# Re-ordering the opening of an adaLN, linear-attention and GLU block: two issuing engines, and the modulation sums of two column blocks on TensorE

## The chip, the cores and the metric

The kernel runs on one core of one Trainium2 chip. The metric is the device time of one execution in microseconds (us), as the median of several runs. Engines are called by their names or as the profile writes them: TensorE (PE for matmuls, PEld for weight loads), VectorE (DVE), ScalarE (ACT), GpSimd (POOL) and SyncE (SP).

## The reference

One transformer block over x of 2048 tokens by 512 columns in float32, with a modulation by a conditioning vector c of 512 numbers:

```
mod = silu(c) @ w_mod                       # 6 x 512: sa, ca, ga, sb, cb, gb
h = layernorm(x) * (1 + ca) + sa
q, k, v = split(h @ wqkv)                   # 32 heads of 16
pq, pk = phi(q), phi(k)                     # phi(t) = (t + 1 if t > 0 else exp(t)) + 1e-6
o = pq (pk^T v) / (pq . sum(pk))            # linear attention, per head
x = x + ga * (o @ wo)
h = layernorm(x) * (1 + cb) + sb
x = x + gb * (((h @ w_gate) * (h @ w_up)) @ w_down)   # inner width 1376
```

The opening, which the change re-orders, covers the layer norm of the first 512 tokens, sa and ca (the "shift" and the "scale" of the first norm), the transposes, the modulation, and the key product of the first four token tiles.

## The kernel before

The 2048 tokens are four chunks of four tiles of 128 tokens. The 512 columns are four blocks of 128 (KD = 4, index k or b). All instructions of an engine run in the order in which the program writes them, and each engine runs its own list; semaphores order them where they share data. DMAs are issued in the program's order by the engine that issues them, and eight completion semaphores are used in turn, so that an issue waits for the transfer eight places ahead of it.

Float32 products are made of two reduced parts. A matrix is split into a high part (a cast on ScalarE) and a low part (the difference, on VectorE), and each product is three matmuls: high by high, high by low, low by high.

The opening goes like this:

- SyncE issues, in this order, x tile 0, c (`ct`), x tiles 1 to 3, the first halves (column blocks 0 and 1) of scale and shift of `w_mod`, the first key weight, the second halves (column blocks 2 and 3), the other three key weights, then x of chunk 1 and the weights of q and v. Each of these tiles is 256 KB, and c is 2 KB. In `raw_half[v, half]`, v = 1 is the scale and v = 0 the shift.
- TensorE has nothing to do until the first tokens are normed. `keep_on(n)` gives it n matmuls of 128x512 on zeros into `ps_idle`, which nobody reads.
- `silu` makes `sc` from c. `n0.stats`, `rstd_of`, `nmr_of` and `xhat` norm the four token tiles (VectorE, a power on GpSimd, then ScalarE or VectorE).
- `transpose_token(j)` turns token tile j, one matmul for each column block, into the four banks `n0.ps[k]`.
- The column sums of silu(c) by `w_mod` are made in one of two ways for each column block b. `block_pe(v, b)` is four matmuls with one output column, accumulated over the four rows of c. `half_dve(v, half, ...)` sums the four pieces on VectorE for two blocks at once, and then `block_one(v, b)` sums over the partitions by one matmul against ones. `block_out(b)` adds 1 to the scale's column and brings the two columns of block b to SBUF. A one-column matmul stands as two records in the profile.
- `mod_h(k)` and `mod_f(k)` (ScalarE) make the high part and the float32 form of the modulated block k from `n0.ps[k]`, and `mod_l(k)` (VectorE) the low part. `weight_h(k)` and `weight_l(k)` split the key weight of row block k. `k_split_xh` and `k_split_xl` split the normed tokens, which are wanted later by `t_tile`.
- `cells((t, k), ..., parts=...)` is the key product: token tile t, row block k, and which of the three matmuls (part 0 high by high, 1 the weight's low part, 2 the tokens' low part). There are 48 in all, L444.

Behind `cells` stands `proj(0, wq)` (its first matmul is L211), and from there on the kernel is a long list of products. The lines of the profile that belong to these steps: L154 `keep_on`, L283 `transpose_token`, L393 `block_pe`, L170 and L172 the sums of `half_dve`, L404 `block_one`, L408 `block_out`, L415 `mod_h`, L422 `mod_f`, L427 `mod_l`, L432 `weight_h`, L435 `weight_l`, L242 `stats`, L254 the power of `rstd_of`, L259 `nmr_of`, L269 `xhat`.

Of the kernel before, what the change touches and what calls it, by code (L numbers as in the profile page):

```python
# [9 lines left out]
F32R = mybir.dt.float32r  # L10
AF = mybir.ActivationFunctionType
# [3 lines left out]
P = 128  # L15
# [7 lines left out]
def tile_adaln_block(  # L23
# [12 lines left out]
    nc = tc.nc  # L36
# [3 lines left out]
    KD = D // P  # L40
    NJ = 4
# [8 lines left out]
    xv = x[0].rearrange("(c p j) d -> c j p d", p=P, j=NJ)  # L50
# [14 lines left out]
    def f32(ap):  # L65
        return ap.bitcast(F32)
# [3 lines left out]
    def T(p, tag, shape=(P, D), dt=F32, bufs=None):  # L70
        cnt[0] += 1
        return p.tile(list(shape), dt, tag="t" if p is tiles else tag, name=f"{tag}_{cnt[0]}", bufs=bufs)

    def B(tag, shape=(P, D), dt=F32):

        return T(tiles, tag, shape, dt)

    def acc_bank():
        return T(ps_acc, "acc")

    def bank():
        return T(ps_w, "bank")
# [23 lines left out]
    nc.gpsimd.memset(half, -0.5)  # L106


    def load(src, tag):
        raw = B(tag, (P, *src.shape[1:]))[:src.shape[0]]  # L110
        nc.sync.dma_start(raw, src)
        return raw

    def load_x(ch):
        return [load(xv[ch, j], "x") for j in range(NJ)]

    def load_mod(v):
        return [load(wm_v[:, k, v * D:(v + 1) * D], "raw") for k in range(KD)]

    def load_half(v, half):  # L120
        a = v * D + half * D // 2
        return [load(wm_v[:, k:k + 2, a:a + D // 2], "raw") for k in range(0, KD, 2)]
# [3 lines left out]

    xts = [[load(xv[0, 0], "x")]]
    ct = consts.tile([P, KD], F32, name="ct")
    nc.sync.dma_start(ct, c[0].rearrange("(p k) -> p k", k=KD))
    xts[0] += [load(xv[0, j], "x") for j in range(1, NJ)]  # L130
    raw_half = {}
    raw_half[1, 0] = load_half(1, 0)
    raw_half[0, 0] = load_half(0, 0)
    load_k = lambda k: load(wqkv_v[k, :, D:2 * D], "raw")
    raw_k = [load_k(0)]
    raw_half[1, 1] = load_half(1, 1)
    raw_half[0, 1] = load_half(0, 1)
    raw_k += [load_k(k) for k in range(1, KD)]
    xts.append(load_x(1))
    raw_q = load_qkv(0)  # L140
    raw_v = load_qkv(2)
# [8 lines left out]
    ps_idle = T(ps_acc, "acc")  # L150

    def keep_on(n):
        for _ in range(n):
            nc.tensor.matmul(ps_idle, idle[:, :P], idle, start=True, stop=True)  # L154
# [3 lines left out]
    sc = consts.tile([P, KD], F32, name="sc")  # L158
# [8 lines left out]
    def mod_acc(acc, raws, ks):  # L167
        for k in ks:
            if k == 0:
                nc.vector.tensor_scalar(acc, raws[k], sc[:, 0:1], None, op0=ALU.mult)  # L170
            else:
                nc.vector.scalar_tensor_tensor(acc, raws[k], sc[:, k:k + 1], acc, op0=ALU.mult, op1=ALU.add)  # L172
# [133 lines left out]
    def proj(i, w, of=bank):  # L306

        ch, j = divmod(i, NJ)
        ps = of()
        product(ps, [(cut(norm[ch].t[k], j * P, (j + 1) * P), w[k]) for k in range(KD)])  # L310
        return ps
# [9 lines left out]
    def k_split_xh(i):  # L321
        ch, j = divmod(i, NJ)
        kx[i] = [B("xh", dt=F32R), B("xl", dt=F32R)]
        nc.scalar.activation(kx[i][0], norm[ch].n[j], AF.Copy)

    def k_split_xl(i):
        ch, j = divmod(i, NJ)
        nc.vector.tensor_tensor(kx[i][1], norm[ch].n[j], f32(kx[i][0]), op=ALU.subtract)
# [45 lines left out]
    n0 = norm[0]  # L374
    both = consts.tile([P, KD, 2], F32, name="both")
    ca, sa = both[:, :, 0], both[:, :, 1]
    ps_m = acc_bank()

    def half_of(v, b):

        pair = raw_half[v, b // 2]
        return [pair[k // 2][:, k % 2, b % 2 * P:(b % 2 + 1) * P] for k in range(KD)]

    def at_of(v, b):
        return 2 * b + 1 - v

    def sums_in(b):
        return ps_idle if b == 1 else ps_m

    def block_pe(v, b):  # L390
        at, ps = at_of(v, b), sums_in(b)
        for k, raw in enumerate(half_of(v, b)):
            nc.tensor.matmul(ps[:, at:at + 1], raw, sc[:, k:k + 1], start=k == 0, stop=k == KD - 1)  # L393

    sums = {}

    def half_dve(v, half, *ks):
        if 0 in ks:
            sums[v, half] = B("f")[:, :D // 2]
        mod_acc(sums[v, half], [raw_half[v, half][k // 2][:, k % 2] for k in range(KD)], ks)  # L400

    def block_one(v, b):
        at = at_of(v, b)
        nc.tensor.matmul(sums_in(b)[:, at:at + 1], sums[v, b // 2][:, b % 2 * P:(b % 2 + 1) * P], ones,  # L404
                         start=True, stop=True)

    def block_out(b):
        nc.vector.tensor_tensor(both[:, b], sums_in(b)[:, 2 * b:2 * b + 2], unit, op=ALU.add)  # L408

    halves = {}  # L410

    def mod_h(k):
        halves[k] = (B("h", dt=F32R), B("h", dt=F32R), B("f"))
        h, l, f = halves[k]
        nc.scalar.activation(h, n0.ps[k], AF.Identity, scale=ca[:, k:k + 1], bias=sa[:, k:k + 1])  # L415

    def mod_f(k, on=None):
        h, l, f = halves[k]
        if on:
            on.tensor_scalar(f, n0.ps[k], ca[:, k:k + 1], sa[:, k:k + 1], op0=ALU.mult, op1=ALU.add)  # L420
        else:
            nc.scalar.activation(f, n0.ps[k], AF.Identity, scale=ca[:, k:k + 1], bias=sa[:, k:k + 1])  # L422
        n0.ps[k] = None

    def mod_l(k):
        h, l, f = halves.pop(k)
        nc.vector.tensor_tensor(l, f, f32(h), op=ALU.subtract)  # L427
        n0.t[k] = (h, l)

    def weight_h(k):  # L430
        wk.append((B("w", dt=F32R), B("w", dt=F32R)))
        nc.scalar.activation(wk[k][0], raw_k[k], AF.Copy)  # L432

    def weight_l(k, on=None):
        (on or nc.vector).tensor_tensor(wk[k][1], raw_k[k], f32(wk[k][0]), op=ALU.subtract)  # L435
# [3 lines left out]
    def cells(*tk, parts=(0, 1, 2)):  # L439
        for part in parts:  # L440
            for t, k in tk:
                h, l = halves[k][:2] if k in halves else n0.t[k]
                x, w = ((h, wk[k][0]), (h, wk[k][1]), (l, wk[k][0]))[part]
                nc.tensor.matmul(kps[t], x[:, t * P:(t + 1) * P], w, start=k == 0 and part == 0,  # L444
                                 stop=k == KD - 1 and part == 2)
# [7 lines left out]
    n0.stats(2)  # L453
    n0.nmr_of(0, 2)
    n0.xhat(0, 1)
    k_split_xh(0)
    n0.stats(3)
    n0.rstd_of(2, 4)
    n0.transpose_token(0)
    n0.nmr_of(2, 4)  # L460
    n0.xhat(2)
    n0.xhat(3, on=nc.vector)
    keep_on(2)
    n0.transpose_token(1)
    block_pe(1, 0)
    keep_on(1)
    half_dve(0, 0, 0, 1, 2, 3)
    weight_h(0)
    n0.transpose_token(2)
    n0.transpose_token(3)  # L470
    keep_on(2)
    block_one(0, 0)
    block_out(0)
    weight_l(0)
    mod_h(0)
    mod_f(0)
    block_pe(1, 1)
    block_one(0, 1)
    half_dve(1, 1, 0, 1)
    block_out(1)  # L480
    half_dve(1, 1, 2, 3)
    mod_l(0)
    kps.update({t: acc_bank() for t in range(2)})
    kps[2] = ps_idle
    kps[3] = bank()
    four = lambda k: [(t, k) for t in range(NJ)]
    cells((0, 0), (1, 0), parts=(0, 1))
    cells((2, 0), (3, 0), parts=(0, 1))
    cells(*four(0), parts=(2,))
    mod_h(1)  # L490
    mod_f(1)
    weight_h(1)
    half_dve(0, 1, 0, 1, 2, 3)
    weight_l(1)
    mod_l(1)
    k_split_xh(1)
    cells(*four(1), parts=(0,))
    block_one(1, 2)
    block_one(0, 2)
    block_one(1, 3)  # L500
    block_one(0, 3)
    cells(*four(1), parts=(1, 2))
    weight_h(2)
    block_out(2)
    block_out(3)
    weight_l(2)
    mod_h(2)
    mod_f(2)
    weight_h(3)
    mod_l(2)  # L510
    mod_h(3)
    weight_l(3)
    mod_f(3)
    k_split_xl(0)
    mod_l(3)
    cells((0, 2), (1, 2))
    cells((2, 2))
    cells((0, 3))
    cells((3, 2))
    cells((1, 3))  # L520
    cells((2, 3))
    cells((3, 3))
    k_split_xl(1)
    nx = Norm(xts[1])

# [18 lines left out]
    ps_m = None  # L544
# [75 lines left out]
    for i in range(4, NT):  # L620
        ch, j = divmod(i, NJ)
# [122 lines left out]
    ps = proj(6, wq)  # L744
# [35 lines left out]
    ps = proj(8, wq)  # L780
# [8 lines left out]
    ps = proj(9, wq)  # L789
# [5 lines left out]
    ps = proj(10, wq)  # L795
# [3 lines left out]
    ps = bank()  # L799
# [583 lines left out]
    for n, (s, g, f) in enumerate(order):  # L1383
# [7 lines left out]
        at = {p: list(early.get((n, p), ())) for p in ("a11", "s1", "s2", "s3", "mid", "s4", "pe")}  # L1391
# [140 lines left out]
```

## Time and profile before

| what | value |
|---|---|
| median of 3 runs | 556.27 us (556.25 to 557.45) |
| the profiled execution, its own time | 557.03 us |
| its span, first to last instruction | 555.0 us |
| busy: TensorE, VectorE, ScalarE, GpSimd | 547.7, 420.4, 296.0, 178.3 us |
| mean granted TensorE clock | 0.998 |
| moved by DMA | 83.75 MB |

The span is the stretch between the first and the last instruction of the profiled execution; its own time has about 2 us around that. The busy times are unions over one engine. In a timeline row, the columns are the start and the length in us, the engine, the line of the kernel, the operation, the tiles (output, then inputs), the shapes, how many instructions are merged into the row, and in brackets the idle time ahead of it and what ended it. In a row by stretch, the first number after the stretch is its length, then for each engine (PE, PEld, DVE, ACT, POOL, or TensorE alone) its busy time with the number of instructions, then the granted clock, the share of the DMA engines, and GB/s.

### The profile page before, as it was taken

The numbers are of one execution on the slowest core, as the hardware profiler recorded it, in microseconds if no ns is written. First come the engines' busy times: TensorE is split into PE (matmuls) and PEld (weight loads), VectorE is DVE, ScalarE is ACT, GpSimd is POOL, SyncE is SP. The second block draws the span as 40 slices with busy tenths as digits, with TensorE's granted clock in tenths as the row PEclk, the third lists the DMA queues.
The fourth block names the chain that finished last, engine by engine and source line by source line (L and its number), as shares of the span: only waits on it lengthen the run. The fifth ranks groups of instructions, "written<-read, shape, count | busy, mean of one in ns | idle before, by whom it ended". The sixth has DMA issues, their size and how long they took to land.

```text
span 555.0 us, 8026 instructions
## 1 busy us (share of the span) xinstructions
PE 547.7 (99%) x2739; PEld 459.8 (83%) x2739; DVE 420.4 (76%) x758; ACT 296.0 (53%) x525; POOL 178.3 (32%) x183
## 2 busy tenths in 40 slices
PE   8999999999999999999999999999999999999996
PEld 6788888888888888888888888878888888888886
DVE  5968779978898998865655767854567878778695
ACT  3876858546467876653545355432443535443540
POOL 2000000002627646343556644400512524242400
PEclk9999999999999999999999999999999999999999
DMA  8910224203230045185888635499585534342004
GB/s 261 384 38 1 76 77 151 78 0 77 77 115 2 0 149 192 39 298 196 284 283 268 227 123 199 154 379 327 176 275 178 185 119 146 131 147 72 0 1 152
DMA packets 56888, 83.75 MB, mean 151 GB/s; under 512 B 6736, under 2 KB 21840, under 8 KB 56848
## 3 DMA queue, kind: packets, MB, share of 16 engines
q1 hardware_dynamic: 56848, 83.26, 43.9%
q8 instruction: 21, 0.34, 0.2%
q14 instruction: 19, 0.16, 0.1%
HBM read 53.54 MB, written 29.69 MB: 150 GB/s over the span
## 4 chain that ended last, share of the span: by engine, by line
PE 96%; DMA 1%; DVE 1%; SPq 0%; issue 0%; ACT 0%; POOL 0%; DVEq 0%
PE bank L1023 38%; PE acc L1182 8%; PE acc L837 8%; PE bank L211 5%; PE bank L213 5%; PE bank L212 5%; PE acc L1106 4%; PE acc L1105 4%; PE acc L1107 4%; PE acc L362 3%; PE acc L361 3%; PE acc L360 3%; PE bank L276 2%; PE acc L444 1%; PE bank L812 1%; DMA x<-in_A_x_dram 1%
## 5 line engine op out<-in xcount | busy, mean ns | idle before, releaser
L1023 PE MATMUL bank<-h,w 128*128 128x512 f32 (+1 forms) x924 | 220.5, 392 | 0.0
L1023 PEld LDWEIGHTS bank<-h,w 128*128 128x128 f32 (+1 forms) x924 | 168.8, 186 | 36.5 <-issue 0.4
L1029 ACT ACTIVATE bank<-bank 128x512 f32<-128x512 f32 (+1 forms) x45 | 26.2, 581 | 131.3 <-PE bank L1023 131.0
L986 POOL TENSOR_TENSOR w<-raw,w 128x256 fp32r<-128x256 f32 (+3 forms) x22 | 24.2, 1099 | 79.7 <-ACT w L979 64.9
L1206 DVE TENSOR_TENSOR x<-acc,x 128x256 f32<-128x256 f32 x108 | 39.2, 414 | 10.5 <-PE acc L1182 9.9
L1182 PE MATMUL acc<-w,kh 128*128 128x256 f32 x252 | 46.8, 283 | 0.0
L211 PE MATMUL bank<-w,h 128*128 128x512 f32 x112 | 44.1, 394 | 0.0
L1182 PEld LDWEIGHTS acc<-w,kh 128*128 128x128 f32 x252 | 41.4, 191 | 3.1 <-DVE x L1206 0.2
L213 PE MATMUL bank<-w,h 128*128 128x512 f32 x112 | 43.7, 390 | 0.0
L212 PE MATMUL bank<-w,h 128*128 128x512 f32 x112 | 43.7, 390 | 0.0
L837 PE MATMUL acc<-w,xh 128*128 128x512 f32 x128 | 40.7, 399 | 0.0
L254 POOL TENSOR_TENSOR rstd<-ve,half 128x4 f32<-128x4 f32 (+3 forms) x12 | 11.2, 930 | 82.7 <-DVE ve L251 71.2
L1049 DVE TENSOR_TENSOR phi<-bank,g 128x512 f32<-128x512 f32 (+1 forms) x22 | 15.1, 687 | 29.8 <-PE bank L1023 28.3
L686 POOL TENSOR_TENSOR f<-h,zb 128x512 f32<-128x512 f32 x12 | 17.5, 1475 | 62.2 <-ACT zb L666 48.8
L1079 DVE TENSOR_TENSOR g<-bank,u 128x512 f32<-128x512 f32 (+1 forms) x22 | 15.2, 690 | 28.0 <-ACT u L1029 26.7
L1106 PE MATMUL acc<-w,kh 128*128 128x512 f32 (+1 forms) x92 | 35.9, 391 | 0.0
L1105 PE MATMUL acc<-w,kh 128*128 128x512 f32 (+1 forms) x92 | 35.9, 391 | 0.0
L1107 PE MATMUL acc<-w,kl 128*128 128x512 f32 (+1 forms) x92 | 35.8, 390 | 0.0
L1182 PE MATMUL acc<-w,kl 128*128 128x256 f32 x126 | 35.7, 283 | 0.0
L1029 ACT ACTIVATE u<-bank 128x512 f32<-128x512 f32 (+1 forms) x44 | 26.2, 594 | 12.6 <-PE bank L1023 12.4
L1112 DVE TENSOR_TENSOR x<-acc,x 128x512 f32<-128x512 f32 x44 | 28.0, 680 | 6.2 <-PE acc L1107 6.2
L269 ACT ACTIVATE n<-x,nmr,rstd 128x512 f32<-128x512 f32 x31 | 23.6, 808 | 14.2 <-DVE nmr L259 14.0
(195 smaller groups left out, 1186.8 us busy)
## 6 DMA issues: line engine op xcount, KB each, us to landing
right<-w SPq DMA_DIRECT2D x56, 256.0 KB, 3.8
w<-right SPq DMA_DIRECT2D x56, 256.0 KB, 3.7
x<-in_A_x_dram SPq DMA_DIRECT2D x24, 256.0 KB, 5.3
raw<-in_w_mod_dram SPq DMA_DIRECT2D x24, 256.0 KB, 3.6
raw<-in_B_w_down_dram SPq DMA_DIRECT2D x20, 256.0 KB, 3.1
side_s<-h SPq DMA_DIRECT2D x16, 256.0 KB, 2.8
h<-side_s SPq DMA_DIRECT2D x16, 256.0 KB, 6.0
raw<-in_A_wqkv_dram SPq DMA_DIRECT2D x12, 256.0 KB, 5.4
```

What stands on the lines that cost most here:

```text
L211: nc.tensor.matmul(ps, ah, bh, start=begin and i == 0, stop=False)
L212: nc.tensor.matmul(ps, ah, bl, start=False, stop=False)
L213: nc.tensor.matmul(ps, al, bh, start=False, stop=end and i == n - 1)
L837: nc.tensor.matmul(yps[i], x, y, start=fresh and k + n == 0, stop=k == KD - 1 and n == 2, skip_group_check=True)
L1023: mm = lambda x, y, **kw: nc.tensor.matmul(ps, x[:, k], y, skip_group_check=True, **kw)
L1029: nc.scalar.activation(out, x, AF.Copy)
L1105: nc.tensor.matmul(dn[j], hh[:n, a:b], dh[:n], start=i == 0, stop=False)
L1106: nc.tensor.matmul(dn[j], hh[:n, a:b], dl[:n], start=False, stop=False)
L1107: nc.tensor.matmul(dn[j], hl[:n, a:b], dh[:n], start=False, stop=i == n_of - 1)
L1112: nc.vector.tensor_tensor(xt, dn[j], xt, op=ALU.add)
L1182: mm = lambda x, y, **kw: nc.tensor.matmul(ps, x[:, a:b], y, skip_group_check=True, **kw)
L1206: nc.vector.tensor_tensor(xt[:, halves[at]], banks[b][:, part], xt[:, halves[at]], op=ALU.add)
```

## The change

- c and x tiles 1 and 3 are issued by ScalarE; x tile 2 and everything else by SyncE.
- The second key weight is issued ahead of the second half of the shift.
- For column block 0 the shift is summed by `block_pe` instead of `half_dve` and `block_one`; for block 1 too, and its four matmuls stand behind the first four cells. All sums go to the bank `ps_m`.
- The unread matmuls behind the first eighteen are three instead of five: one between the transposes of tokens 0 and 1, two ahead of `block_pe(1, 1)` and the first product.
- The transposes of tokens 3 and 2 stand behind the sums of block 0.
- The order of the casts, splits and cells behind that is another: `k_split_xh` comes later, `block_one` of blocks 2 and 3 is split around the second part of k = 1, both `mod_h` of blocks 2 and 3 come ahead of both `mod_f`, and the cells of k = 2 and 3 are ordered by part.
- `mod_h` gets a range of columns, of which only the whole is used.

```diff
-    def load(src, tag):
+    def load(src, tag, by=None):
         raw = B(tag, (P, *src.shape[1:]))[:src.shape[0]]
-        nc.sync.dma_start(raw, src)
+        (by or nc.sync).dma_start(raw, src)
         return raw
...
-    nc.sync.dma_start(ct, c[0].rearrange("(p k) -> p k", k=KD))
-    xts[0] += [load(xv[0, j], "x") for j in range(1, NJ)]
+    nc.scalar.dma_start(ct, c[0].rearrange("(p k) -> p k", k=KD))
+    xts[0] += [load(xv[0, j], "x", by=nc.sync if j == 2 else nc.scalar) for j in range(1, NJ)]
...
     raw_half[1, 1] = load_half(1, 1)
+    raw_k += [load_k(1)]
     raw_half[0, 1] = load_half(0, 1)
-    raw_k += [load_k(k) for k in range(1, KD)]
+    raw_k += [load_k(k) for k in range(2, KD)]
...
     def sums_in(b):
-        return ps_idle if b == 1 else ps_m
+        return ps_m
...
-            nc.tensor.matmul(ps[:, at:at + 1], raw, sc[:, k:k + 1], start=k == 0, stop=k == KD - 1)
+            nc.tensor.matmul(ps[:, at:at + 1], raw, sc[:, k:k + 1], start=k == 0, stop=k == KD - 1,
+                             skip_group_check=True)
...
     n0.xhat(0, 1)
-    k_split_xh(0)
     n0.stats(3)
     n0.rstd_of(2, 4)
     n0.transpose_token(0)
+    keep_on(1)
+    n0.transpose_token(1)
+    block_pe(1, 0)
+    block_pe(0, 0)
     n0.nmr_of(2, 4)
     n0.xhat(2)
     n0.xhat(3, on=nc.vector)
+    block_out(0)
+    weight_h(0)
+    n0.transpose_token(3)
+    n0.transpose_token(2)
     keep_on(2)
-    n0.transpose_token(1)
-    block_pe(1, 0)
-    keep_on(1)
-    half_dve(0, 0, 0, 1, 2, 3)
-    weight_h(0)
-    n0.transpose_token(2)
-    n0.transpose_token(3)
-    keep_on(2)
-    block_one(0, 0)
-    block_out(0)
+    block_pe(1, 1)
+    mod_h(0)
+    half_dve(1, 1, 0, 1)
     weight_l(0)
-    mod_h(0)
     mod_f(0)
-    block_pe(1, 1)
-    block_one(0, 1)
-    half_dve(1, 1, 0, 1)
-    block_out(1)
     half_dve(1, 1, 2, 3)
     mod_l(0)
+    weight_h(1)
...
-    cells((0, 0), (1, 0), parts=(0, 1))
-    cells((2, 0), (3, 0), parts=(0, 1))
-    cells(*four(0), parts=(2,))
+    cells(*four(0), parts=(0,))
+    block_pe(0, 1)
+    block_out(1)
+    cells(*four(0), parts=(1, 2))
     mod_h(1)
+    weight_l(1)
     mod_f(1)
-    weight_h(1)
-    half_dve(0, 1, 0, 1, 2, 3)
-    weight_l(1)
+    half_dve(0, 1, 0)
     mod_l(1)
+    half_dve(0, 1, 1, 2, 3)
+    weight_h(2)
+    weight_h(3)
+    k_split_xh(0)
     k_split_xh(1)
     cells(*four(1), parts=(0,))
     block_one(1, 2)
+    block_one(1, 3)
+    cells(*four(1), parts=(1,))
     block_one(0, 2)
-    block_one(1, 3)
     block_one(0, 3)
-    cells(*four(1), parts=(1, 2))
-    weight_h(2)
+    cells(*four(1), parts=(2,))
     block_out(2)
     block_out(3)
     weight_l(2)
     mod_h(2)
+    mod_h(3)
     mod_f(2)
-    weight_h(3)
+    weight_l(3)
+    k_split_xl(0)
     mod_l(2)
-    mod_h(3)
-    weight_l(3)
     mod_f(3)
-    k_split_xl(0)
     mod_l(3)
-    cells((0, 2), (1, 2))
-    cells((2, 2))
-    cells((0, 3))
-    cells((3, 2))
-    cells((1, 3))
-    cells((2, 3))
-    cells((3, 3))
+    cells(*four(2), parts=(0, 1))
+    for t in range(NJ):
+        cells((t, 3), parts=(0, 1))
+        cells((t, 2), (t, 3), parts=(2,))
```

More of the change, by code (lines that the diff above doesn't have):

```diff
@@ L410, in tile_adaln_block, with mod_h @@
     halves = {}
[L412 to L415, printed above, removed]
+    def mod_h(k, a=0, b=NJ):
+        if not a:
+            halves[k] = (B("h", dt=F32R), B("h", dt=F32R), B("f"))
+        h = halves[k][0][:, a * P:b * P]
+        nc.scalar.activation(h, n0.ps[k][:, a * P:b * P], AF.Identity, scale=ca[:, k:k + 1], bias=sa[:, k:k + 1])
     def mod_f(k, on=None):
```

## The prediction

> **What bounds the kernel now.** I read the page's span and busy line first, then the busy time by stretch, then TensorE's timeline of the first 30 us, and the other engines' timelines only where TensorE was late.
>
> ```profile
> span 555.0 us, 8026 instructions
> PE 547.7 (99%) x2739; PEld 459.8 (83%) x2739; DVE 420.4 (76%) x758; ACT 296.0 (53%) x525; POOL 178.3 (32%) x183
> 5.00:6.00 1.00, 1.00 (x4) 0.71 (x4) 0.89 (x4) 0.00 (x0) 0.00 (x0) 1.00 0.71 204
> ...
> 11.00:12.00 1.00, 0.66 (x5) 0.41 (x5) 0.96 (x3) 0.54 (x1) 0.00 (x0) 1.00 1.09 351
> 30.00:35.00 5.00, 5.00 (x24) 4.14 (x23) 3.74 (x11) 1.86 (x4) 1.01 (x1) 1.00 0.00 1
> ```
>
> TensorE is busy for 547.7 of 555.0 us, and from the first full stage on (30 to 35 us: 5.00 of 5.00) it never waits. The change touches nothing behind that, so the question is only when TensorE reaches `proj(0, wq)`, the first L211. Its opening:
>
> ```profile
> 1.98 6.58 PE L154 MATMUL acc<-w 128*128 128x512 f32 x18 [1.98 <-DVE w L149]
> 8.56 0.66 PE L283 MATMUL bank<-ident,n 128*128 128x128 f32 x4
> ...
> 9.53 0.60 PE L283 MATMUL bank<-ident,n 128*128 128x128 f32 x4
> 9.96 0.95 PE L393 MATMUL acc<-sc,raw 128*128 128x1 f32 x8
> 10.78 0.47 PE L154 MATMUL acc<-w 128*128 128x512 f32 x1
> 11.60 1.09 PE L283 MATMUL bank<-ident,n 128*128 128x128 f32 x8 [0.34 <-ACT n L269]
> 12.45 0.71 PE L154 MATMUL acc<-w 128*128 128x512 f32 x2
> 13.24 0.35 PE L404 MATMUL acc<-ones,f 128*128 128x1 f32 x2
> 13.46 1.03 PE L393 MATMUL acc<-sc,raw 128*128 128x1 f32 x8
> 14.35 0.36 PE L404 MATMUL acc<-ones,f 128*128 128x1 f32 x2
> 14.66 1.43 PE L444 MATMUL acc<-w,h 128*128 128x512 f32 x5
> ...
> 16.38 0.39 PE L444 MATMUL bank<-w,h 128*128 128x512 f32 x1
> 16.89 0.97 PE L444 MATMUL acc<-w,h 128*128 128x512 f32 x3
> ...
> 18.84 0.95 PE L404 MATMUL acc<-ones,f 128*128 128x1 f32 x8
> 19.65 0.94 PE L444 MATMUL acc<-w,h 128*128 128x512 f32 x3
> ...
> 27.20 0.39 PE L211 MATMUL bank<-w,h 128*128 128x512 f32 x1
> ...
> 29.92 0.39 PE L360 MATMUL acc<-kh,xh 128*128 128x512 f32 x1
> ```
>
> The first useful matmul (L444, `cells`) starts at 14.66, L211 at 27.20: 12.54 us for the 48 matmuls of `cells`. Spacing: twelve matmuls from 27.20 to 29.92, 0.227 each. One `block_pe` (four matmuls, two records each) takes 0.82 to 0.89 (9.96 to 10.78, 13.46 to 14.35), four `block_one` 0.81 (18.84 to 19.65), four transposes 0.43 (9.53 to 9.96), eight 0.85 (11.60 to 12.45). So 12.54 is 48 x 0.227 = 10.9, plus 0.81, plus 0.8 of lost time; one loss is visible, 16.38 to 16.89, 0.28 beyond the spacing.
>
> What sets 14.66:
>
> ```profile
> 1.24 0.42 SPq L129 DMA_DIRECT2D ct<-in_c_dram  x1
> 1.71 1.37 SPq L111 DMA_DIRECT2D x<-in_A_x_dram  x3
> 5.48 0.69 DVE L242 BATCH_NORM_STATS2 st<-x 128x6 f32<-128x512 f32 x1
> 6.62 0.70 DVE L242 BATCH_NORM_STATS2 st<-x 128x6 f32<-128x512 f32 x1
> 8.60 0.69 DVE L242 BATCH_NORM_STATS2 st<-x 128x6 f32<-128x512 f32 x1 [0.94 <-DMA x<-in_A_x_dram]
> 11.57 1.52 DVE L172 SCALAR_TENSOR_TENSOR f<-raw,sc,f 128x256 f32<-128x256 f32 x3
> 13.63 0.16 DVE L408 TENSOR_TENSOR both<-acc,unit 128x2 f32<-128x2 f32 x1 [0.54 <-PE acc L404]
> 16.15 0.68 DVE L427 TENSOR_TENSOR h<-f,h 128x512 fp32r<-128x512 f32 x1
> 7.69 1.52 ACT L269 ACTIVATE n<-x,nmr,rstd 128x512 f32<-128x512 f32 x2 [3.39 <-DVE nmr L259]
> 12.30 0.63 ACT L432 ACTIVATE w<-raw 128x512 fp32r<-128x512 f32 x1 [0.76 <-DMA raw<-in_A_wqkv_dram]
> 13.83 0.78 ACT L415 ACTIVATE h<-bank,both 128x512 fp32r<-128x512 f32 x1 [0.89 <-DVE both L408]
> 20.03 0.78 ACT L415 ACTIVATE h<-bank,both 128x512 fp32r<-128x512 f32 x1 [1.72 <-DVE both L408]
> 20.70 0.77 ACT L422 ACTIVATE f<-bank,both 128x512 f32<-128x512 f32 x1
> ```
>
> The transposes of block 0 are done at 12.45, but block 0's shift is summed on VectorE until 13.09, crosses L404 and L408, and only then does ScalarE make `h` (13.83 to 14.61).
>
> **The change, part by part.** Tiles by arrival: the second x tile is in by 5.48, the third by 6.62, the fourth at 8.6, the first key weight at 12.3. At 351 GB/s (11 to 12 us) a 256 KB tile takes 0.75, so the tile before that weight, the last half of block 0's shift, lands at about 11.55 (estimate); call it L.
>
> *Shift of block 0 on TensorE.* VectorE loses four sums (the row 1.52 plus one), L404 goes, and `block_pe(0, 0)` stands ahead of the transposes of tokens 3 and 2. From L: its last two matmuls 0.41, eight transposes 0.85, the two unread matmuls about 0.6 (row 12.45), `block_pe(1, 1)` 0.85: first cell at L + 2.7 = 14.25. ScalarE's `h` (0.16 + 0.78 after the transposes) lies beside the pair and those sums (1.45), and `weight_h(0)` is done by 12.93. If that cover went, `h` would cost about 0.9.
>
> *The same from x.* Token 0 was transposed at 8.56, 3.1 after the second x tile (statistics, the power on GpSimd, `n` at 7.69). Then 0.41 + 0.3 + 0.43, both sums 1.7, and 0.85 + 0.6 + 0.85: second x + 8.2. That is 13.7 if it comes by 5.48 and 14.8 if it comes with the third. From the fourth x: 3.0 to the transposes (8.6 to 11.60), then 2.3: 13.9, or 14.65 if it comes one tile later.
>
> *Two issuing engines.* The vector c and the second and fourth x go to ScalarE's queue, ahead of its table load; everything on SyncE moves up by three issues of about 0.45, 1.3 us. I take nearly nothing for it: all of it was issued long before it landed, and the transfers ran at 204 GB/s between 5 and 6 us with the requests already out. The bounds: if the early tiles come at the later 0.75 each, the second x sets the time and the first cell is at about 13.6; if the two queues share the engines, the second x lands with the third and the fourth with the tile behind it: 14.8. I take 14.25, between them. The activation table and `sc` are needed only at 9.9, so three issues ahead of them cost nothing. [...]
>
> *Behind the first cell.* Still 48 matmuls, 10.9. `block_pe(0, 1)` now lies inside, 0.85, beside four `block_one` 0.81. Its `block_out(1)` and `h` (about 1.1) are hidden by eight cells (1.8). The loss at 16.89 goes: `mod_l(0)` is ready at about 16.2 (raw half by 13.05, sums 0.85, `weight_l` 0.6, sums 1.0, itself 0.68), and with eight more records ahead of it TensorE wants it at 16.9. A new one comes. `block_out(2)` was covered by eight cells, now by four: from the end of the `block_one` (19.65) to `h` (20.81) is 1.2 in the rows, the cover 4 x 0.227 = 0.9, so 0.3 lost. ScalarE then makes h, h, f, f at 0.67 each (20.03 to 20.70), and `mod_l(3)` is ready 3.5 after the first h began, TensorE there 3.3 after: 0.2. Together 10.9 + 0.85 + 0.81 + 0.5 = 13.1 against 12.54.
>
> *The rest.* The two `xh` casts move behind the weights; ScalarE waits there anyway (1.72 ahead of 20.03). The second key weight moves two tiles earlier and is wanted later. No cost.
>
> **Sum.** 14.25 + 13.1 = 27.35 against 27.20: +0.15 us, 0.4 gained ahead of the first cell and 0.55 given back behind it. The profiled execution took 557.03 (span 555.0 and 2.0 around it), so 557.2; the median of the runs is 0.76 lower, so 556.4.
>
> **The rivals.** *The early transfers do speed up.* For it, 204 against 351 GB/s. First cell 13.6, end 26.7, -0.5: 555.8. It can't give more: the chain from the statistics to the transposes remains. *The second queue delays x.* First cell 14.8, +0.7: 557.0.
>
> *The clock falls.* This is the one on the slower side.
>
> ```profile
> 2.00:6.40 4.40, 4.40 (x10) 1.00 0.77 232
> 10.10:13.50 3.40, 2.97 (x23) 1.00 1.10 358
> 549.40:552.80 3.40, 0.93 (x8) 1.00 0.70 230
> 552.80:555.00 2.20, 0.00 (x0) 0.50 0.02 6
> ```
>
> The 18 unread matmuls at first took 0.44 each (4.40 for 10), twice the later 0.227, for 4.4 us. At the end the granted clock is 0.50 right after a stretch with 0.93 of 3.40 busy. In before, the longest stretch without a 512-column matmul ahead of the first cell is 10.78 to 12.45; after the change only one stands between token 0 (about 9.0) and the pair (12.8), 3.8 us filled with 12 transposes of 128 columns and 16 records of one column. In columns this is about 1,550; the eight matmuls of 256 columns ahead of the fall make 2,048. If columns count, the clock falls near 13; if any activity counts, it stays, since TensorE is busy for most of it, as in the 2.97 of 3.40 where it stayed. [...] Price: 3.4 (the stretch at the end) to 4.4 us (the start) at 0.44 instead of 0.227, half of it lost: 1.7 to 2.1, end about 558.3. [...]
>
> *The change doesn't do what it says*: the sums on TensorE wait for L just as those on VectorE did. That is in the forecast.
>
> **How the numbers follow.** 0.3% is 1.7 us, about what a measurement of this kernel can tell from no change. Forecast (about +0.15, within 0.5) 0.48; transfers faster (-0.5) 0.14; x delayed (+0.7) 0.10; clock falls (+1.8 to +2.2) 0.22; something no row shows, 0.06, mostly on the faster side, as the clock holds most of the slower one. The first three are all within 0.3%, 0.72; so faster 0.05, same 0.70, slower 0.25, the clock's share and a little of the rest. The range runs from the transfers' rival, 555.5 with the spread of the forecast, to the clock's, 558.2.
>
> **What would show it.** In the profile after: the first cell at 14.2 (13.6 or 14.8 for the transfers' rivals), L211 at 27.3; eight one-column records behind the first four cells; a gap of 0.3 ahead of the first cell of k = 2, none ahead of the low part of k = 0; cells 0.227 apart. I am wrong if the cells stand 0.43 apart or a granted clock of 0.50 shows ahead of 20 us, if the first cell is ahead of 13.4, or if TensorE waits anywhere behind 28 us.

## The result and the profile after

| | median | runs | lowest to highest |
|---|---|---|---|
| kernel before, on the same chip | 556.95 us | 22 | 555.96 to 561.50 |
| kernel after | 558.08 us | 22 | 557.48 to 563.01 |

The ratio is 1.0026, with a 95% interval of 1.0015 to 1.0037. The change costs 0.8 to 2.1 us, where the prediction had +0.15. The kernel before had a median 0.7 above the three runs that the prediction started from, so most of the distance between 556.4 and 558.08 is the change and the rest is that baseline.

Two things are mixed in the 22 runs. Seventeen of them took 557.5 to 558.8 us. In the other five the granted clock of TensorE fell for a time: four took 559.15 to 559.32 us at a mean granted clock of 0.995, and one, the profiled one, 563.01 at 0.989. Of the kernel before, one run of 22 was such a one by its time (561.50). Both things have to be explained, the steady microsecond and the falls.

The page of the profiled execution of after shows the fall in its second slice:

```profile
span 560.9 us, 8042 instructions
PEclk9699999999999999999999999999999999999999
```

By stretch (length, then busy time and number of instructions of PE, PEld, DVE, ACT and POOL, then granted clock, DMA share, GB/s), with stretches of 3.41 us, a third of the time at the lower clock, laid from its edges at 12.53 and 22.77:

```profile
5.70:9.12 3.42, 2.41 (x11) 1.62 (x9) 2.59 (x7) 0.58 (x1) 0.71 (x1) 1.00 1.06 375
9.12:12.53 3.41, 3.12 (x27) 3.00 (x28) 1.10 (x5) 2.27 (x4) 0.70 (x1) 1.00 1.08 362
12.53:15.95 3.42, 3.42 (x17) 3.23 (x15) 3.04 (x7) 1.96 (x3) 0.00 (x0) 0.50 1.07 379
15.95:19.36 3.41, 3.41 (x14) 3.02 (x13) 0.00 (x0) 0.00 (x0) 0.00 (x0) 0.50 1.05 385
19.36:22.77 3.41, 3.41 (x10) 2.79 (x10) 2.22 (x6) 2.71 (x5) 0.00 (x0) 0.50 1.06 387
22.77:26.19 3.42, 3.42 (x20) 2.95 (x19) 1.20 (x5) 0.95 (x3) 0.00 (x0) 1.00 1.05 385
```

The clock is at 0.50 for 10.24 us, and the opening is about 5 us longer than in an unfallen execution (L212 at 32.74, against 27.79 in e1 below): about half of the 10.24. The stretch ahead of the fall has TensorE busy for 3.12 of 3.41 us, more than the stretch before it (2.41), behind which the clock stayed. So in this execution the clock fell behind a stretch that was 91% busy, and stayed behind one of 70%. What fills the former is seen in the timeline of TensorE:

```profile
9.40 0.65 PE L284 MATMUL bank<-ident,n 128*128 128x128 f32 x4 [1.30 <-ACT n L270]
9.81 0.48 PE L155 MATMUL acc<-w 128*128 128x512 f32 x1
10.13 0.64 PE L284 MATMUL bank<-ident,n 128*128 128x128 f32 x4
10.61 1.84 PE L394 MATMUL acc<-sc,raw 128*128 128x1 f32 x16
12.31 1.76 PE L284 MATMUL bank<-ident,n 128*128 128x128 f32 x8
...
16.28 1.63 PE L447 MATMUL acc<-w,h 128*128 128x512 f32 x3
...
32.74 0.39 PE L212 MATMUL bank<-w,h 128*128 128x512 f32 x1
```

In the stretch ahead of the fall stand one wide matmul (512 columns), ten transposes and sixteen one-column records. The first projection (L212 now) is at 32.74, 5.5 later than before. This execution lost another 0.74 us against before's between 133 and 160 us, in three pieces; ahead of the last of them TensorE waits for VectorE, which it never does there in before:

```profile
159.96 0.66 PE L811 MATMUL bank<-ident,h 128*128 128x128 f32 x4 [0.31 <-DVE h L720]
```

The trace mixes several effects, so the steady cost is read from a second profiled execution of the same kernel, in which the clock stayed (e1, mean 0.998):

```profile
5.00:6.00 1.00, 1.00 (x4) 0.71 (x4) 0.63 (x5) 0.00 (x0) 0.00 (x0) 1.00 1.03 327
```

```profile
6.16 0.69 DVE L243 BATCH_NORM_STATS2 st<-x 128x6 f32<-128x512 f32 x1 [0.46 <-DMA x<-in_A_x_dram]
...
9.24 0.66 PE L284 MATMUL bank<-ident,n 128*128 128x128 f32 x4 [0.55 <-ACT n L270]
...
14.32 0.93 PE L447 MATMUL acc<-w,h 128*128 128x512 f32 x3
15.10 0.39 PE L447 MATMUL bank<-w,h 128*128 128x512 f32 x1
15.32 0.95 PE L394 MATMUL acc<-sc,raw 128*128 128x1 f32 x8
16.13 0.96 PE L447 MATMUL acc<-w,h 128*128 128x512 f32 x3
...
17.16 0.85 PE L447 MATMUL acc<-w,h 128*128 128x512 f32 x3
...
19.00 0.50 PE L406 MATMUL acc<-ones,f 128*128 128x1 f32 x4
19.36 0.96 PE L447 MATMUL acc<-w,h 128*128 128x512 f32 x3
...
20.39 0.50 PE L406 MATMUL acc<-ones,f 128*128 128x1 f32 x4
20.75 0.95 PE L447 MATMUL acc<-w,h 128*128 128x512 f32 x3
21.54 0.40 PE L447 MATMUL bank<-w,h 128*128 128x512 f32 x1
21.95 0.97 PE L447 MATMUL acc<-w,h 128*128 128x512 f32 x3
...
23.90 3.14 PE L447 MATMUL acc<-w,h 128*128 128x512 f32 x12
...
27.79 0.39 PE L212 MATMUL bank<-w,h 128*128 128x512 f32 x1
```

First cell 14.32, L212 27.79: the 48 cells take 13.46 us, 0.92 more than before, and the first cell comes 0.34 earlier than in the trace of before. From L212 to the last product, the products of this execution keep that distance of 0.59 us from their partners in before to within 0.05, so the opening alone sets it. The row at 6.16 is the statistics of the second x tile, which landed at 6.14; the first cell is timed from that landing further below.

### The profile page after: what moved, and what is told of

The parts are those of the page before. It is cut to its first block, busy times and chain, and to the rows that moved or that the text cites. A ratio compares the mean times of both kernels' runs of the same rounds, so it can differ in the third digit from the quotient of the medians.

```text
span 560.9 us, 8042 instructions
## 1 busy us (share of the span) xinstructions
PE 552.8 (99%) x2749; PEld 464.3 (83%) x2749; DVE 421.2 (75%) x754; ACT 295.7 (53%) x525; POOL 177.7 (32%) x183
## 4 chain that ended last, share of the span: by engine, by line
PE 92%; DVE 4%; ACT 2%; DMA 1%; issue 0%; POOL 0%; ACTq 0%; DVEq 0%; POOLq 0%
PE bank L1022 38%; PE acc L1181 8%; PE acc L836 8%; PE acc L1104 4%; PE acc L1105 4%; PE acc L1106 4%; PE bank L212 4%; PE bank L214 4%; PE bank L213 4%; PE acc L363 2%; PE acc L361 2%; PE acc L362 2%; PE acc L447 2%; PE bank L277 2%; PE bank L811 1%; DMA x<-in_A_x_dram 1%
## 5 line engine op out<-in xcount | busy, mean ns | idle before, releaser
L212 PE MATMUL bank<-w,h 128*128 128x512 f32 x112 | 44.2, 394 | 0.0
```

The source lines that it names most:

```text
L212: nc.tensor.matmul(ps, ah, bh, start=begin and i == 0, stop=False)
```

## The experiments

All ratios are against the kernel before on the same chip, with the 95% interval. "First cell" and "tail" (first cell to first projection) are of one profiled execution, in which the clock stayed unless said. A run counts as fallen where its mean granted clock is 0.996 or less; unfallen ones have 0.997 to 1.000.

**e1: the kernel after once more.** No edit.

> The kernel after, unchanged, to see how often the granted clock falls in the opening and what is left where it does not. Theory A (second x tile): the opening ends later even at full clock, because the second x tile lands at 6.3 instead of 5.5; first cell at about 14.5, first L212 at about 27.7, runs at full clock about 1 us above the kernel before. Theory B (the clock): nearly every run has a fall, and a run without one is level with the kernel before. Theory C (the work behind the first cell): the first cell stands where it stood (14.66) and the stretch from it to the first L212 is 13.1 or more instead of 12.54.

Measured: 557.66 us, ratio 1.0028 (1.0012 to 1.0044); three of 11 runs fell (559.17, 559.18, 562.57). The eight others have a median of 557.57, 0.8 above before (556.78 on this chip). So the loss is there without the falls, and with the 22 runs above 8 of 33 fell. First cell 14.32, tail 13.46: the rows above.

**e2: after, with all loads on SyncE in the order of before.**

```diff
-    nc.scalar.dma_start(ct, ...)
-    xts[0] += [load(xv[0, j], "x", by=nc.sync if j == 2 else nc.scalar) for j in range(1, NJ)]
+    nc.sync.dma_start(ct, ...)
+    xts[0] += [load(xv[0, j], "x") for j in range(1, NJ)]
```

> The kernel after with all loads issued by SyncE again, in the order of before (x 0, c, x 1 to 3). Theory A: the second x tile is back at 5.5, but the last half of block 0's shift at about 11.5 instead of 9.9; first cell at L + 2.7 = 14.2, 0.3 ahead of the unchanged kernel after, the rest as there. Theory B: no change in the share of runs with a fallen clock, so no change in time beyond 0.3. Theory C: no change, since all of the cost lies behind the first cell.

Measured: 557.81 us, 1.0038 (1.0013 to 1.0062), three of 11 fell; first cell 14.62, tail 13.45. The second x landed at 6.43, although SyncE issued it as in before, where the trace had 5.46:

```profile
6.46 0.69 DVE L243 BATCH_NORM_STATS2 st<-x 128x6 f32<-128x512 f32 x1 [1.05 <-DMA x<-in_A_x_dram]
```

The eight unfallen runs have a median of 557.76, against 557.57 in e1. One queue or two makes no difference that can be told, to the falls neither.

**e3: after, with two more unread matmuls** between the transposes of token 1 and the sums of block 0.

```diff
     n0.transpose_token(1)
     block_pe(1, 0)
+    keep_on(1)
     block_pe(0, 0)
+    keep_on(1)
```

> The kernel after with two more unread matmuls, one behind each of the first two column sums of block 0, so that no stretch longer than about 1.5 us is without a 512-column matmul. Theory B: no run has a fallen clock, and the median goes down by 1 us or more to that of the kernel before. Theories A and C: the runs with a fall go, but the median of the others goes up by 2 x 0.227 = 0.45.

Measured: 558.54 us, 1.0031 (1.0019 to 1.0043), none of five fell. First cell 15.38 with the second x at 6.68: 8.7 behind it instead of 8.2, so each unread matmul costs 0.25. The mean granted clock was 0.998 to 1.000 in these five runs, but for a price in every one.

**e4: after, with the second x ahead of c on ScalarE's queue.**

```diff
+    xts[0] += [load(xv[0, 1], "x", by=nc.scalar)]
     nc.scalar.dma_start(ct, ...)
-    ... for j in range(1, NJ)]
+    ... for j in range(2, NJ)]
```

> The kernel after with the second x tile ahead of c on ScalarE's queue, so that it is issued at 0.8 instead of 1.2. Theory A: it lands 0.4 earlier and everything behind follows, 0.4 faster than the unchanged kernel after; c is later by 0.4 and covered. Theories B and C: no change in time.

Measured: 562.06 us, 1.0116 (1.0075 to 1.0156); four of six fell. A miss. The second x did land earlier, at 5.07, but c, now issued behind it on ScalarE's queue, came at 6.84 instead of 4.34 (e1). Standing behind a tile of 256 KB can't be the whole reason: in before and e2, c stands behind the first x on SyncE's queue, and landed at 4.07 and 4.05. What held it here stays open. Its timeline:

```profile
7.10 0.17 DVE L164 TENSOR_SCALAR ce<-ce 128x4 f32<-128x4 f32 x1 [1.20 <-ACT ce L163]
...
7.52 0.16 DVE L166 TENSOR_TENSOR sc<-ct,ce 128x4 f32<-128x4 f32 x1
7.60 0.69 DVE L244 BATCH_NORM_STATS2 st<-x 128x6 f32<-128x512 f32 x1
```

The statistics of the second x stand behind `sc` in the program and started at 7.60, not at 5.1; first cell 15.75, tail 13.46.

**e5: after, with the pair of unread matmuls parted**, one of them moved between the two sums of block 0.

```diff
     block_pe(1, 0)
+    keep_on(1)
     block_pe(0, 0)
...
-    keep_on(2)
+    keep_on(1)
```

> The kernel after with the same three unread matmuls, but the pair ahead of the first product is split: one stands between the two column sums of block 0, one ahead of block_pe(1, 1). [...] Activity theory (any instruction counts, so the falls come from TensorE's waits): the waits are where they were, and about a quarter of the runs still fall.

Measured: 558.14 us, 1.0015 (1.0006 to 1.0024), none of 11 fell; first cell 14.61, tail 13.44. With the same matmuls in another place the mean granted clock was 0.998 to 1.000 in these runs, at no cost in the profile. At 8 falls in 33, eleven runs without one have a chance of about 0.05, so that the place matters is likely and not certain. What is left is the steady loss.

**e6: after, with block 1's shift summed on VectorE** in pieces of 128 columns, behind which a single matmul against ones replaces the four of `block_pe(0, 1)`.

```diff
+    def quarter_dve(v, b):
+        acc = B("f")[:, :P]
+        mod_acc(acc, half_of(v, b), range(KD))
+        return acc
+    def quarter_one(v, b, acc): ...   # one matmul of acc by ones
...
     n0.xhat(3, on=nc.vector)
+    s01 = quarter_dve(0, 1)
...
-    block_pe(0, 1)
+    quarter_one(0, 1, s01)
```

> The kernel after with block 1's shift summed on VectorE, which is idle there (four pieces of 128 columns, then one matmul against ones where the four of block_pe(0, 1) stood). Theory C (the work behind the first cell): first cell where it was (14.3), the stretch behind it 0.6 shorter, so 0.6 us faster than the unchanged kernel after at full clock. Theory A: no change, if the first cell is what counts. [...]

Measured: 557.45 us, 1.0023 (1.0001 to 1.0045); three of 12 fell (561.42 to 561.99). First cell 14.60. The tail is 12.76, 0.7 shorter:

```profile
15.40 0.40 PE L456 MATMUL bank<-w,h 128*128 128x512 f32 x1
15.63 0.28 PE L416 MATMUL acc<-ones,f 128*128 128x1 f32 x2
15.77 0.93 PE L456 MATMUL acc<-w,h 128*128 128x512 f32 x3
...
27.37 0.39 PE L212 MATMUL bank<-w,h 128*128 128x512 f32 x1
```

0.14 us stands where 0.81 stood in e1 (15.32 to 16.13). That is the larger part of the steady loss. The nine unfallen runs have a median of 557.33, 0.3 above before's 557.03, where e1 stood 0.8 above. The profiled run itself took 557.97, the longest of the nine: it lost 0.76 us between 133 and 167 us, as after's did.

**e7: the kernel before with two issuing engines, and nothing else of the change.** The edit is the first two pieces of the change's diff.

> The kernel before with only the two issuing engines of the change (c and x tiles 1 and 3 by ScalarE). Theory A (the second queue delays the second x tile): about 0.3 to 0.8 slower than before. Against it, from the runs so far: the second x tile lands at 6.1 to 6.7 with one queue and with two, and the weights 1.1 to 1.6 earlier with two, so the same time as before or 0.3 faster. No fall of the clock in either, since all five unread matmuls stand.

Measured: 556.92 us, 0.9998 (0.9989 to 1.0006), none of 11 fell; first cell 14.50, tail 12.57, second x at 6.21. Two queues alone do nothing to the time of before.

**e8: the kernel before with three unread matmuls instead of five.**

```diff
-    keep_on(2)
+    keep_on(1)
     n0.transpose_token(1)
     block_pe(1, 0)
-    keep_on(1)
```

> The kernel before with three unread matmuls behind the first eighteen instead of five (one between tokens 0 and 1, none behind the first column sums, two ahead of the first block's sum). [...] Activity theory: no fall, as in before, since TensorE's waits are as short.

Measured: 557.11 us, 1.0001 (0.9992 to 1.0009), none of 11 fell; first cell 14.85, tail 12.54. The number of unread matmuls alone is not the cause: with as many of them, 8 of 33 runs of after fell.

**e9: after, with block 0's scale summed ahead of the first token's transposes**, while TensorE waits for that token.

```diff
+    block_pe(1, 0)
     n0.transpose_token(0)
     keep_on(1)
     n0.transpose_token(1)
-    block_pe(1, 0)
     block_pe(0, 0)
```

> The kernel after, with one step moved: the column sums of block 0's scale (eight one-column matmuls, 0.89 us) go ahead of the first token's transposes, into the 1.2 us in which TensorE waits for that token. Theory (the opening is bound by TensorE from the first token on): first cell 0.9 us earlier at the same landings, 13.3 to 13.8 instead of 14.32; tail still 13.45; unfallen runs at 556.7, level with the kernel before (ratio 0.999 to 1.001). [...] Rival (the landing of block 0's last shift half and the chain behind it set the first cell): first cell within 0.2 of 14.32, time 557.5.

Measured: 557.30 us, 0.9995 (0.9977 to 1.0013), one of 11 fell.

```profile
8.25 1.02 PE L394 MATMUL acc<-sc,raw 128*128 128x1 f32 x8
9.61 0.66 PE L284 MATMUL bank<-ident,n 128*128 128x128 f32 x4 [0.34 <-ACT n L270]
...
13.80 0.96 PE L447 MATMUL acc<-w,h 128*128 128x512 f32 x3
```

From token 0 to the first cell there are 4.19 us instead of 5.08 (9.24 to 14.32): all of the 0.89. So TensorE, from the first token on, sets the first cell of after, and the landing of the shift does not. The tail is 13.47, unchanged. The ten unfallen runs have before's own unfallen median, 557.21.

**e10: after without its three unread matmuls.**

```diff
     n0.transpose_token(0)
-    keep_on(1)
     n0.transpose_token(1)
...
-    keep_on(2)
     block_pe(1, 1)
```

> The kernel after without its three unread matmuls behind the first 18. [...] Any-activity theory: TensorE is occupied by one-column matmuls just as long, no run falls, first cell 0.3 to 0.5 earlier, median 557.1. A chance fall that has nothing to do with the kernel: the same share as before it, under 3 in 10.

Measured: 562.00 us, 1.0065 (1.0036 to 1.0093); nine of 12 fell (560.13 to 564.50), the other three took 557.04 to 557.45. By stretch, and TensorE's timeline, of a fallen one:

```profile
8.60:12.01 3.41, 2.41 (x20) 2.17 (x21) 1.71 (x6) 2.85 (x4) 0.70 (x1) 1.00 1.08 361
12.01:15.42 3.41, 3.41 (x19) 3.41 (x18) 2.30 (x6) 1.21 (x3) 0.00 (x0) 0.50 1.07 372
15.42:18.84 3.42, 3.42 (x14) 3.03 (x13) 0.78 (x2) 0.76 (x2) 0.00 (x0) 0.50 1.06 388
18.84:22.25 3.41, 3.41 (x11) 2.88 (x11) 1.84 (x5) 2.29 (x4) 0.00 (x0) 0.50 1.05 387
22.25:25.66 3.41, 3.41 (x12) 2.78 (x10) 1.25 (x3) 1.24 (x3) 0.00 (x0) 0.50 1.05 387
```

```profile
9.55 1.36 PE L284 MATMUL bank<-ident,n 128*128 128x128 f32 x8 [1.72 <-ACT n L270]
10.75 2.26 PE L394 MATMUL acc<-sc,raw 128*128 128x1 f32 x16
```

From 9.55 on TensorE is busy without a gap, and only its wide matmuls were taken away; the falls went from 8 of 33 to 9 of 12. Two stretches have the same busy time: the first row here, 2.41 us of transposes and one-column records, was followed by 0.50, and the first row of after's profile (5.70 to 9.12), 2.41 us of 512-column matmuls, by 1.00. So busy time alone does not tell when the clock falls; between these two it is the work that differs. The three unfallen runs have a median of 557.32, 0.1 above before, so the unread matmuls cost time, and with them fewer runs fell.

**e11: after, with the shift sums of blocks 2 and 3 in one piece** and their matmuls beside those of the scale.

```diff
-    half_dve(0, 1, 0)
-    mod_l(1)
-    half_dve(0, 1, 1, 2, 3)
+    half_dve(0, 1, 0, 1, 2, 3)
+    mod_l(1)
...
-    cells(*four(1), parts=(1,))
     block_one(0, 2)
     block_one(0, 3)
-    cells(*four(1), parts=(2,))
+    cells(*four(1), parts=(1, 2))
```

> The kernel after with the shift sums of blocks 2 and 3 made in one piece on VectorE and their two ones-matmuls put beside those of the scale, behind part 0 of k = 1 (one switch back to wide cells fewer, and mod_h(2) covered by eight cells). Theory (the tail is longer by the switches and by the stalls ahead of k = 2 and k = 3, 0.5 in all): tail 12.9 instead of 13.46, unfallen runs 557.1. Rival (VectorE isn't ready with the sums there, and TensorE waits instead): tail 13.3 to 13.6, time as the kernel after, 557.6. Falls as in the kernel after, 2 to 4 in 11, since the opening up to the first cell is the same.

Measured: 557.66 us, 1.0005 (0.9988 to 1.0022); two of 11 fell. First cell 14.63. The tail is 12.88:

```profile
19.30 0.95 PE L406 MATMUL acc<-ones,f 128*128 128x1 f32 x8
20.11 0.96 PE L447 MATMUL acc<-w,h 128*128 128x512 f32 x3
...
23.88 2.88 PE L447 MATMUL acc<-w,h 128*128 128x512 f32 x12
```

One switch back to wide cells is gone, and the twelve cells at 23.88 take 2.88 instead of 3.14: no stall at k = 3. Together with the 0.70 of e6 these 0.58 make 1.28, more than the 0.92 by which e1's tail is longer than before's. The nine unfallen runs have a median of 557.56, 0.35 above before.

**e12: all moves in one.** The edits of e6, e9 and e11 together, and those of the unread matmuls from e5 (one behind token 1, one ahead of `block_pe(1, 1)`).

> All in one, from the kernel after: block 0's scale sums ahead of the first token, block 1's shift sums on VectorE with a single ones-matmul, the sums of blocks 2 and 3 together, and one of the two paired unread matmuls put between the second token and block 0's shift sums. Theory (each gain adds): first cell 13.3 to 13.8, tail 12.1 to 12.3, first projection at 25.5 to 26.0 instead of 27.2 in the kernel before, no falls: 555.3 to 555.7, ratio 0.9975. Rival (a head start is given back later, as 0.75 us between 134 and 166 us in e6 and e7's profiled runs): ratio 0.999 to 1.000.

Measured: 555.62 us (555.10 to 556.13), ratio 0.9965 (0.9951 to 0.9980), none of 11 fell. It is faster than both kernels: its longest run is shorter than the shortest of any version of after.

```profile
6.42 2.82 PE L155 MATMUL acc<-w 128*128 128x512 f32 x8
9.07 0.95 PE L394 MATMUL acc<-sc,raw 128*128 128x1 f32 x8
9.88 0.64 PE L284 MATMUL bank<-ident,n 128*128 128x128 f32 x4
...
14.03 0.94 PE L456 MATMUL acc<-w,h 128*128 128x512 f32 x3
...
15.04 0.28 PE L416 MATMUL acc<-ones,f 128*128 128x1 f32 x2
...
26.20 0.39 PE L212 MATMUL bank<-w,h 128*128 128x512 f32 x1
```

Tail 12.17, which is 13.46 less the 0.70 of e6 and the 0.58 of e11: the gains add. The first cell, at 14.03, missed its expectation by 0.2: the last eight of the eighteen unread matmuls took 2.65 us (6.42 to 9.07, 0.33 each, where the last seven of e9 took 0.23 each) and ran into the sums, and token 0 was transposed at 9.88 although, 3.1 behind the second x at 6.49, it would have been ready at 9.6.

## Why the prediction was wrong

**What bounds the kernel: right in the main.** What the opening loses is lost at the end: in ten of the thirteen other profiles the products keep their distance from before's, within 0.1, from L212 on. In three (after, e6, e7) another 0.75 us goes between 133 and 160 us, where TensorE once waits 0.31 for VectorE. The prediction held such a wait for a sign of being wrong. It isn't the steady loss, as e1 has that without it.

**Two issuing engines: right, at nothing** (e7 0.9998, e2 as e1). The early transfers did run faster, 327 GB/s between 5 and 6 us (e1) instead of 204 (before), but what that brought early was the weights. The second x, which counts, landed between 6.14 and 6.68 in all ten traces with the change's loads, and at 5.46 (before), 5.65 (e8) and 6.43 (e2) with before's. So the landings don't exclude that two queues delay it, as one of the rivals had it; the times speak against it, since in after the first cell follows the second x, and e2 with one queue is no faster than e1. The prediction took the 5.46 of one trace as the kernel's.

**The first cell: right number, wrong path, so luck.** 14.25 was forecast as L + 2.7 with L about 11.55. L came at 10.03 in e1, so that path would have given 12.7. The other path of the same paragraph, second x + 8.2, is the one that holds: 6.14 and 14.32 in e1, 6.42 and 14.61 in e5, 6.45 and 14.63 in e11; e9 shortened just this chain. As before's trace has a late L (11.59) and an early x, the "0.4 gained ahead of the first cell" compared two different bounds. At like arrival of x the gain is about 0.1 (e7 14.50 with x at 6.21, e1 14.32 with 6.14).

**Behind the first cell: the term that was mis-sized.** 13.1 was forecast and 13.46 measured, at the same 13.43 to 13.47 in e1 to e5 and e9. The 0.85 for `block_pe(0, 1)` and the 0.81 for the four `block_one` came out at 0.81 and 0.73 (two pairs of 0.36 and 0.37), and the cover lost ahead of k = 2 and 3 is there (0.41 between 21.54 and 21.95, and 3.14 instead of 2.88 for the twelve cells at 23.90: 0.18 and 0.26 lost). What was left out is what each return to wide matmuls costs: the three cells behind a group of one-column matmuls or a stall take 0.93 to 0.97, against 0.85 elsewhere, so 0.1 each, and after has five of them (14.32, 16.13, 19.36, 20.75, 21.95), where before had three (14.66, 16.89, 19.65). With the 0.44 of the stalls this makes 13.4. The prediction had this loss before it: it found 0.8 of lost time in before's 12.54, put 0.28 of it down to a stall, and carried nothing of the other 0.5 into the sum for after, without a reason. Three returns make 0.3 of that 0.5; the rest was not traced. The steps that eight cells hide `block_out(1)`, and that the low part of k = 0 no longer waits, were right. So the balance of +0.15 is about +0.8 at full clock, 0.1 gained and 0.9 given back. Of the 0.65 between the two, about 0.3 is the gain ahead of the first cell that isn't there, and about 0.35 the tail.

**The clock: a rival at 0.22, and it is part of the result.** Eight of 33 runs fell; that this share is near the 0.22 is chance, since the 0.22 was for the whole kernel and not for a share of its runs. It was weighed as an alternative to the forecast, while it happens beside the steady loss, in some runs. "If columns count, the clock falls near 13; if any activity counts, it stays": it fell at 12.53 in the trace, behind a stretch that was busy for 3.12 of 3.41 us, so activity alone did not keep it; that columns are what counts was the author's estimate, and no run shows it. The price was sized rightly, or a little high, for four of the five falls of after (1.7 to 2.1; they stood 1.2 to 1.4 above the 557.9 of the unfallen). But the 3.4 us in it was the length of a stretch ahead of the lower clock at the end of before, and no trace shows a fall of that length: in the two traces with a fall in the opening the clock was at 0.50 for 10.24 us (after) and through all the 13.65 us from 12.01 to 25.66 (e10), and these runs, at 563.01 and 563.50, are 5.1 and 6.2 us longer than the unfallen ones of their kernels. That a fall can last was not foreseen; what makes it last stays open.

**The range** of 555.5 to 558.2 held the median of after, and that is luck: its upper end was made for a kernel whose clock falls, and the median run's did not. The chance of 0.70 for no change and the sign of its forecast (+0.15, within 0.5) did not allow for a steady +0.8.

**What stays open** is what makes the clock fall. It fell behind 3.12 of 3.41 us busy in after and behind 2.41 in e10, and stayed behind 2.41 in after; with three unread matmuls it fell in 8 of 33 runs of after, and in none of the 11 of e8 nor of the 11 of e5, where they stand in other places. Of the three falls of before in 115 runs no trace was kept.

## What to carry to other kernels

Where TensorE is the bound from some point on, as here, an operation put between its products can be paid in full, however small its output: the one-column sums of `block_pe(0, 1)` cost 0.81 us in e1, and each return to the wide matmuls about 0.1 more. Put it where TensorE waits anyway (e9, e12), or let another engine do its larger part (e6, 0.14 instead of 0.81). Look at the granted clock where TensorE does transposes and one-column work, as it fell behind such stretches in after and e10; with the unread wide matmuls parted (e5) none of 11 runs fell, against 8 of 33. Count several runs, since the fall came in some only. And take arrival times from several traces before a chain is built on one of them: the second x landed at 5.46 and at 6.43 us under the same order of loads.

## What the runs showed of the hardware

- The granted clock fell to 0.50 behind a stretch in which TensorE was busy for 3.12 of 3.41 us, and rose again 10.24 us later (after). Of two stretches with 2.41 us busy, it stayed at 1.00 behind the one with 512-column matmuls (after) and fell to 0.50 behind the one with transposes and one-column records (e10).
- In e1 the 512-column matmuls behind one-column ones or behind a stall lost about 0.1 us at the start: 0.93 to 0.97 for three cells instead of 0.85.
- The same load order brought the second x in at 5.46 (before), 5.65 (e8) and 6.43 us (e2).
- The 2 KB of c landed at 4.34 us (e1, issued at 0.80), 4.07 (before, issued at 1.24) and 6.84 (e4, issued at 1.23 behind the second x on ScalarE's queue).
- Between 133 and 167 us, which no kernel here touches, the profiled runs of after, e6 and e7 lost 0.74 to 0.76 us against before's, at the same three places, and the ten others less than 0.1. What sets it off stays open.
